# Score and activation matmuls as chained 64-row halves, banks by name, score copies on ScalarE

## The chip, the cores and the metric

The kernel runs on one core of one Trainium2 chip. The metric is the device time of one execution in microseconds, the median of three runs. The profiled execution is a run of its own. It has a span, from the first to the last instruction, and its own time, which takes in what lies around the span.

## The reference, cut to what matters

Two branches over the same input x (2048 tokens, 576 features) are mixed by a gate. Branch a is a long convolution with a kernel K that is generated from complex parameters (576 channels, 128 states). Branch b is a product-key expert layer: scores of 32 heads against 2 x 64 keys, the two best of each, a softmax over the two best pairs, and for the chosen experts a GELU of x·u, which weighs rows of v.

```python
g = sigmoid((x * gate_w).sum(-1, keepdims=True))
# a: K[d, l] = Re sum_n C dt B exp(l dt A);  y = irfft(rfft(u) * rfft(K))[:L] + u * Dskip
# b: 4096 experts = 64 x 64
s1 = einsum("nhd,ed->nhe", q1, k1); s2 = einsum("nhd,ed->nhe", q2, k2)
i1, i2 = two best of s1, two best of s2
top_s, top_e = two best of the four sums t1 + t2
act = gelu(einsum("nd,nhkd->nhk", x, u[top_e]))
b = einsum("nhk,nhk,nhkd->nd", softmax(top_s), act, v[top_e])
out = g * a + (1 - g) * b
```

## The kernel before

The program is written out by a planner: a model clock advances with each matmul that `mm` (L214) records, generators for every side task lie on a heap and are run by `pump` when their time has come, and `ready` and `need` make them wait for a modelled result or a free buffer. The order in which instructions are recorded is the order of each engine's queue. ScalarE and VectorE calls go through `Engine.call` (L134), so almost every row names one of those two lines.

**Score groups** (`s`, 128 of them). The key matrices are folded into the query weights, which gives 4096 score columns. A group is one of 8 column blocks of 512 by one of 16 tiles of 128 tokens. Both operands are split into a high and a low fp16 part (three products: high-high, high-low, low-high). `triple` records four contraction steps of 128 rows with three products each, and two matmuls for the last 64 features, whose high and low parts are stacked in one 128-row operand; half of the second one's rows are zero. That is 14 matmuls of 512 columns in one accumulation bank. `scores_top` then runs 8 MAX8 and 8 FIND_INDEX8 on VectorE, straight from the bank.

**Activation groups** (`a`, 128 of them) are the same for x·u: 8 blocks of 512 experts, 4 token blocks, 4 parts. `act_post` scales the bank into `go` and stores it.

The main loop takes a score group when VectorE's modelled lag is small enough and a bank is free, otherwise an activation group. It holds the last 26 activation groups back while score groups remain.

**The second path** runs beside it. `k_params`, `k_factors` (wbp), `k_front` (kP, phases), `k_gen` (kb) and `k_store` make the convolution kernel, 16 channels at a time. `u_stage1` makes the first stage of the input's transform, `k_stage1` (k) that of the kernel, `products` (pr, pi, pv) multiplies in the frequency domain. Then `gating` and `v_work` (vhl, the split expert table) finish what the output stage needs.

**The output stage.** For each token tile `prep` builds one-hot matrices on VectorE, PE places the gates (S), and 192 matmuls of 288 columns (o) sum over the experts; `y_part` adds the convolution.

**Banks.** There are eight accumulation banks. `bank` takes a place from a quota (sc for groups, kb and wb for the second path) and a tile from one ring of eight:

```python
def bank(tag, name):
    take(tag, name)
    t = ps.tile([128, 512], F32, tag="ps", name=name, bufs=8)
```

At the start the quotas are sc=4, kb=4; after the kernel generation sc=4, wb=4; during the products sc=3, wb=5. All DMAs are issued by SyncE in recorded order.

Of the kernel before, what the change touches and what calls it, by code (L numbers as in the profile page):

```python
# [18 lines left out]
OP = mybir.AluOpType  # L19
# [19 lines left out]
KB = 4  # L39
RA = 2 * CH * R1  # L40
# [98 lines left out]
def body(ctx: ExitStack, tc: tile.TileContext, xT, au, par, logdt, dskip, gatew, wq, kT, uT, vv,  # L139
# [67 lines left out]
    def mm(o, l, r, start, stop, cost=None):  # L207
        m = l.shape[0] > 64, 128 if size(l) > 64 else size(l)
        if m != tiling[0]:
            tiling[0] = m  # L210
            clock[0] += 0.13 if m == (True, 128) else 0.1
        clock[0] += (size(r) * (4 if r.dtype == F32 else 1) / 2400 + 0.003) if cost is None else cost
        rdy[key(o)] = clock[0] + 0.4
        T.matmul(o, l, r, start=start, stop=stop)  # L214
# [26 lines left out]

    def wait(gen):
        for t in gen:
            idle(t)

    slots, caps, owed = {}, {}, {}

    def quota(**kw):
        for tag, n in kw.items():
            lst = slots.setdefault(tag, [])  # L250
# [10 lines left out]
    def need(tag, n=1):  # L261
        while True:
# [10 lines left out]
    def free(tag, *outs):  # L273
# [14 lines left out]
    quota(sc=4, wb=0, kb=4, hw=1, slot=9, go=3, m8=2, raw=1, ko=1)  # L288
# [153 lines left out]
    def squares(a, r, sq, dst):  # L442
# [8 lines left out]
        mm(p[:, 0:2], onesb, short(acc[0].start, 2), True, True, 0.05)  # L451
        yield from ready(p)
        V.tensor_reduce(out=dst, in_=p[:, 0:2], axis=AX, op=OP.add)
        free(tag, dst)
# [5 lines left out]
    def x_norm(tb, sq):  # L460
# [15 lines left out]
        free("kb", nx)  # L476
# [23 lines left out]
    def scale_first(a, r, sq, keep=None):  # L500
# [16 lines left out]
        free("kb", out[0])  # L517
        return out

    def x_build(tb):  # L520
# [32 lines left out]
        V.scalar_tensor_tensor(b[64:128, 8], r[64:128], s[64:128], b[64:128, 8], op0=OP.mult, op1=OP.subtract)  # L553
        free("slot", b)
        xb.append(b)
        if tb == 3:
            V.tensor_reduce(out=nx2, in_=nx, axis=AX, op=OP.max)
            yield from ready(nx2)
            open_u()
# [38 lines left out]
    def w_half(c, h, w):  # L598
# [17 lines left out]
        for n in range(2):  # L616
            mm(p[:, 0:1], onesb, short(acc[n].start, 1), n == 0, n == 1, 0.03)
# [3 lines left out]
        free(tag, s)  # L621
# [19 lines left out]
    def w_tail(c, k, pb, hl, rem, o, count, s, tag):  # L641
        yield from ready(pb, s)
        if k < 4:
            yield from split(hl[:, 0, k:k + 2, o], hl[:, 1, k:k + 2, o], pb.rearrange("p (k n) -> p k n", k=2), s)
            free(tag, hl)
        else:
# [5 lines left out]
            for ps_, co in halves2:  # L652
                V.scalar_tensor_tensor(rem[0:64, 1, co], pb[ps_, 0:128], s[ps_], rem[ps_, 0, co],
                                       op0=OP.mult, op1=OP.subtract)
            free(tag, rem)
# [29 lines left out]
    def k_params():  # L685
# [7 lines left out]
        Zp = kg.tile([128, NCK, 6, CH], BF16, name="Zp")  # L693
# [74 lines left out]
        for h in range(2):  # L768
# [5 lines left out]
            free("kb", sc[:, b[h]])  # L774
# [5 lines left out]
        par_t.update(g=gN, a=aN, rt=rt[:, 0:RA // 2].bitcast(BF16), l2=rt[:, RA // 2:RA // 2 + R2], l1=rt[:, RA // 2 + R2:], Z=Zp)  # L780
# [4 lines left out]
    def k_factors(g):  # L785
# [3 lines left out]
        for k in range(KB):  # L789
            mm(p[:6 * CH, NS * k:NS * k + NS], par_t["Z"][:, KB * g + k], identb, True, True)  # L790
        yield from ready(p)
        t = kg.tile([6 * CH, KB, NS], BF16, tag="wb", name=f"wb{g}", bufs=2)
        copy(t.rearrange("p k n -> p (k n)"), p[:6 * CH])
        free("kb", t)
# [6 lines left out]
    def k_front(c):  # L801
# [18 lines left out]
        def reduce(z, p):  # L820
# [9 lines left out]
            free("kb", CS)  # L830
            left[0] -= 1

        for z in range(2):
# [4 lines left out]
            mm(p, wb_[:, c % KB, :], rt[0:6 * CH, 512 * z:512 * z + 512], True, True)  # L838
            spawn(reduce(z, p))
# [18 lines left out]
        for CS, e, ex in both:  # L858
            S.activation(e, e, AF.Exp)
            S.activation(ex, ex, AF.Exp)  # L860
        for d, (CS, e, ex) in enumerate(both, c - 1):
            v = CS.rearrange("p c s l -> p s c l")
            S.activation(v[:, 0:2], v[:, 0:2], AF.Sin, scale=-TWO_PI, bias=halfpi)
            S.activation(v[:, 2:4], v[:, 2:4], AF.Sin, scale=-TWO_PI)
# [48 lines left out]
    def k_store(c, kb):  # L913
# [9 lines left out]
        free("kb", ko)  # L923
# [4 lines left out]
        if kstored[0] == NCK:  # L928
# [3 lines left out]
            quota(sc=4, wb=4, kb=0, raw=2)  # L932
# [16 lines left out]

    tops = {}  # L950

    def scores_top(c, t, pb):
        yield from ready(pb)
        q = t % 4
        if q == 0:
            yield from need("m8")
            take("m8", "m8")
            tops[c, t // 4] = (xp.tile([128, 4, 8, 8], F32, tag="m8", name=f"m8_{c}_{t}", bufs=2),
                               xp.tile([128, 4, 8, 8], U32, tag="i8", name=f"i8_{c}_{t}", bufs=2))
        while (c, t // 4) not in tops:  # L960
            yield 0.3
        m8, i8 = tops[c, t // 4]
# [4 lines left out]
        free("sc", i8)  # L967
        seen[0] += 1
        if q == 3:
            yield from ready(i8)  # L970
            S.activation(vals[:, t - 3:t + 1, 8 * c:8 * c + 8, :], m8[:, :, :, 0:2], AF.Copy)
            S.activation(idx[:, t - 3:t + 1, 8 * c:8 * c + 8, :], i8[:, :, :, 0:2], AF.Copy)
# [71 lines left out]
    def turned(t, p):  # L1044
# [3 lines left out]
        free("wb", idxT)  # L1048
# [14 lines left out]
    def u_stage1():  # L1063
# [18 lines left out]
        def tail(p, tag, pbs):  # L1082
            for g in range(2):
                o = us[:, 2 + g, :]
                for hh in range(2):
                    pb = pbs[hh][g]
                    yield from ready(pb)
                    ov = o[:, 288 * hh:288 * hh + 288]
                    S.activation(ov, pb[:, :288], AF.Copy)
                    free(tag, ov)  # L1090
                yield from ready(ov)
                dma(pair_rows(su_d, 2 * p + g), o)
            ended[0] += 1

        load(0)
        for p in range(NT):
# [4 lines left out]
            h = uf.tile([128, 2, D], F16, tag="uh", name=f"uh{p}", bufs=2)  # L1101
# [10 lines left out]
            yield from need(tag, 4)  # L1112
            hungry[0] = False
            pbs = [[bank(tag, f"u1_{p}_{g}_{hh}") for g in range(2)] for hh in range(2)]
            for hh in range(2):
                cs = slice(288 * hh, 288 * hh + 288)
                for n, (z, w) in enumerate(((0, 0), (0, 1), (1, 0))):
                    for g in range(2):
                        r = slice(64 * g, 64 * g + 64)
                        mm(pbs[hh][g][:, :288], tu[r, z], h[r, w, cs], n == 0, n == 2, 0.063)  # L1120
            spawn(tail(p, tag, pbs))
            del pbs
# [11 lines left out]
    def k_stage1(ksb, fk, tabs):  # L1134
        enter, leave, count = ring(3)

        def tail(w, o, pbs):
# [702 lines left out]
```

## Time and profile before

| | |
|---|---|
| median of three runs | 1455.22 us (1452.94 to 1456.87) |
| profiled execution, own time | 1458.63 us |
| its span | 1456.8 us, 36814 instructions |
| PE busy | 1430.8 us (98%) |
| DVE busy | 1221.0 us (84%) |
| ACT busy | 776.0 us (53%) |
| POOL busy | 521.4 us (36%) |
| mean granted TensorE clock | 0.998 of 2.4 GHz |

An engine's busy time is the union of its instructions' records. A matmul's record is longer than its share of the engine, because matmuls are pipelined; the pitch from one start to the next tells what it costs. "A x12" in a timeline is a run of twelve records, its second number the time from the first start to the last end.

### The profile page before, as it was taken

The numbers are of one execution on the slowest core, as the hardware profiler recorded it, in microseconds if no ns is written. First come the engines' busy times: TensorE is split into PE (matmuls) and PEld (weight loads), VectorE is DVE, ScalarE is ACT, GpSimd is POOL, SyncE is SP. The second block draws the span as 40 slices with busy tenths as digits, with TensorE's granted clock in tenths as the row PEclk, the third lists the DMA queues.
The fourth block names the chain that finished last, engine by engine and source line by source line (L and its number), as shares of the span: only waits on it lengthen the run. The fifth ranks groups of instructions, "written<-read, shape, count | busy, mean of one in ns | idle before, by whom it ended". The sixth has DMA issues, their size and how long they took to land.

```text
span 1456.8 us, 36814 instructions
## 1 busy us (share of the span) xinstructions
PE 1430.8 (98%) x14103; PEld 853.9 (59%) x14105; DVE 1221.0 (84%) x4569; ACT 776.0 (53%) x1304; POOL 521.4 (36%) x510
## 2 busy tenths in 40 slices
PE   7999999999999999999999999999899999999998
PEld 3445445555454445455555444447687887888787
DVE  6898889889877996885989898689998988998860
ACT  6346776796685776834556564576333224323310
POOL 0335357536446446210237999623000100110100
PEclk9999999999999999999999999999999999999999
DMA  8235223442434432269486776787343432342400
GB/s 306 77 112 172 88 80 109 126 138 72 129 106 124 116 104 92 62 211 292 157 304 216 266 250 214 255 265 228 130 122 110 140 120 98 125 148 67 157 9 17
DMA packets 134352, 215.44 MB, mean 148 GB/s; under 512 B 10912, under 2 KB 79904, under 8 KB 127776
## 3 DMA queue, kind: packets, MB, share of 16 engines
q1 hardware_dynamic: 134080, 213.01, 45.3%
q8 instruction: 111, 1.82, 0.5%
q14 instruction: 65, 0.53, 0.1%
q10 hardware_dynamic: 96, 0.07, 0.0%
HBM read 141.74 MB, written 71.30 MB: 146 GB/s over the span
## 4 chain that ended last, share of the span: by engine, by line
PE 85%; DVE 5%; DMA 2%; ACT 1%; issue 0%; POOL 0%; SPq 0%; DVEq 0%; POOLq 0%
PE o L214 25%; PE s L214 22%; PE a L214 22%; PE S L214 4%; PE kb L214 2%; PE wb L214 2%; PE pr L214 2%; DMA vn<-in_au_dram 1%; PE y L214 1%; PE kP L214 1%; PE k L214 1%; DVE i L134 1%; PE pv L214 1%; PE u L214 1%; DVE vhl L134 1%; DVE m L134 1%
## 5 line engine op out<-in xcount | busy, mean ns | idle before, releaser
L214 PE MATMUL o<-vhl,wh 128*128 128x288 f16 x3072 | 389.2, 287 | 0.0
L214 PE MATMUL s<-whl,xb 128*128 128x512 f16 x1536 | 365.0, 379 | 0.0
L214 PE MATMUL a<-xb,uhl 128*128 128x512 f16 x1536 | 359.5, 379 | 0.2 <-DVE go L134 0.2
L214 PEld LDWEIGHTS <-wh 128*128 128x128 f16 x3072 | 296.8, 98 | 77.5 <-issue 3.7
L214 PEld LDWEIGHTS <-xb 128*128 128x128 f16 x1792 | 170.6, 98 | 208.5 <-issue 14.3
L214 PEld LDWEIGHTS <-uhl 128*128 128x128 f16 x1536 | 147.1, 98 | 176.3 <-issue 3.2
L134 DVE FIND_INDEX8 i<-m,s 128x8 uint32<-128x64 f32 x1024 | 206.9, 226 | 0.0
L134 ACT ACTIVATE wh<-gl,s_wg 128x1024 f16<-128x1024 f32 x64 | 69.0, 1137 | 203.6 <-DVE gl L134 203.6
L134 DVE MAX8 m<-s 128x8 f32<-128x64 f32 x1024 | 146.4, 217 | 27.1 <-PE s L214 26.6
L134 POOL TENSOR_TENSOR CS<-CS,ex 128x512 f32<-128x512 f32 x72 | 97.9, 1389 | 147.6 <-DVE ex L134 146.2
L134 POOL TENSOR_TENSOR ya<-ya,db 128x576 f32<-128x576 f32 x16 | 31.8, 1995 | 320.3 <-DVE Bg L134 159.2
L134 ACT ACTIVATE go<-a,i_a 128x512 f32<-128x512 f32 x92 | 61.5, 682 | 89.1 <-PE a L214 63.9
L134 DVE TENSOR_TENSOR gl<-S,gl 128x256 f32<-128x256 f32 x256 | 90.3, 416 | 13.5 <-PE S L214 10.1
L134 POOL TENSOR_TENSOR e<-aN,rt 128x512 f32<-128x512 f32 x72 | 83.1, 1174 | 49.9 <-PE kb L214 43.8
L134 DVE SCALAR_TENSOR_TENSOR wh<-gl,s_wg,wh 128x1024 f16<-128x1024 f32 x64 | 91.1, 1455 | 11.3 <-ACT wh L134 11.3
L134 DVE TENSOR_TENSOR Bg<-Be,vals 128x1024 f16<-128x1024 f16 x128 | 91.7, 758 | 2.2
L134 ACT ACTIVATE gl<-gl 128x1024 f32<-128x1024 f32 x64 | 63.4, 1044 | 34.1 <-DMA gl<-g_d 34.1
L214 PE MATMUL S<-Bg,A 128*128 128x64 f16 x2048 | 73.6, 194 | 6.4 <-DVE Bg L134 6.4
L214 PEld LDWEIGHTS <-A 128*128 128x128 f16 x2048 | 71.4, 98 | 11.4 <-DVE Bg L134 4.9
L134 DVE TENSOR_TENSOR A<-iota_a,vals 128x2048 f16<-128x2048 f16 x64 | 77.9, 1218 | 0.0
L134 DVE MATCH_VALUE_LOAD i<-m,s 128x8 f32 x1024 | 76.3, 75 | 0.1
L214 PE MATMUL s<-wrem,xb 128*128 128x512 f16 x256 | 76.2, 379 | 0.0
(206 smaller groups left out, 2156.6 us busy)
## 6 DMA issues: line engine op xcount, KB each, us to landing
g_d<-go SPq DMA_DIRECT2D x128, 256.0 KB, 2.4
gl<-g_d SPq DMA_DIRECT2D x32, 1024.0 KB, 5.5
wq<-in_wq_dram SPq DMA_DIRECT2D x16, 1152.0 KB, 5.6
su_d<-us SPq DMA_DIRECT2D x32, 288.0 KB, 2.6
sk_d<-k1o SPq DMA_DIRECT2D x32, 288.0 KB, 3.7
vn<-in_vv_dram SPq DMA_DIRECT2D x32, 288.0 KB, 4.1
ui<-su_d SPq DMA_DIRECT2D x16, 576.0 KB, 4.0
ki<-sk_d SPq DMA_DIRECT2D x16, 576.0 KB, 5.5
```

The source lines that it names most:

```text
L134: return f(*a, **k)
L214: T.matmul(o, l, r, start=start, stop=stop)
```

## The change

Score and activation groups are recorded as two lists of 64-row matmuls: the upper 64 partitions and the lower 64 (27 together). A queue `upper` and a list `lower` are served in ticks by `row_slot`: one matmul of an upper half, then one of a lower half of an earlier group. Both halves of a group add into the same bank. The lower half may start once more than LAG = 3 ticks have gone by since its upper half's last matmul, and an explicit wait for that matmul stands ahead of it. Consecutive groups alternate between even and odd token blocks, whose remainder part lies in opposite halves (14 + 13 and 13 + 14).

```diff
+    def row_slot():
+        tick[0] += 1
+        cost = 0.0
+        if upper:
+            g = upper[0]
+            o, l, r, start, stop = g["up"].popleft()
+            cost = size(r) / 2400 + 0.003
+            g["last"] = mm(o, l, r, start, stop, cost)
+            if not g["up"]:
+                upper.popleft()
+                g["end"] = tick[0]
+                lower.insert(sum(x["short"] for x in lower) if g["short"] else len(lower), g)
+        now = [g for g in lower if tick[0] - g["end"] > LAG or not upper]
+        if now:
+            g = now[0]
+            o, l, r, start, stop = g["low"].popleft()
+            if g["last"] is not None:
+                tc.add_manual_dep(T.nop().ins, g["last"].ins.name, ...)
+                g["last"] = None
+            mm(o, l, r, start, stop, max(0.0, size(r) / 2400 + 0.003 - cost))
...
+    def halved(pb, hl, rem, x, tb, tok, cols, x_first):
+        parts = []
+        for z in range(2):
+            h = slice(64 * z, 64 * z + 64)
+            lst = []
+            for k in range(4):
+                for xk, w in ((k, 0), (k, 1), (4 + k, 0)) if x_first else ((k, 0), (4 + k, 0), (k, 1)):
+                    lst.append((x[h, xk, tok], hl[h, w, k, cols]))
+            for n in range(1 + (z == tb % 2)):
+                lst.append((x[h, 8, tok], rem[h, n, cols]))
```

The remainder's low part is now written to all 128 partitions, so `w_tail` does four subtractions of 64x128 where it did two, and `u_build` one over 128 partitions.

Other matmuls go through the same queue as short groups ahead of the others (`first=True`): the norm sums (`total`: sq, wn), the factor transposes (wbp), the phases kP (96 rows before, 128 rows now, half each) and the stage k. They are done when their lower half is.

```diff
-                for n in range(2):
-                    mm(pb[:, :288], tkt[:, w % 16, n], ksb[:, 2 * hh:2 * hh + 2, :, w, :]..., n == 0, n == 1)
+                gs.append(rows(*([(pb[:, :288], tkt[h:h + 64, w % 16, n],
+                                   ksb[h:h + 64, 2 * hh:2 * hh + 2, :, w, :]...,
+                                   h == 0 and n == 0, h == 64 and n == 1) for n in range(2)] for h in (0, 64)), first=True))
```

Banks have names: each of the eight is a tile of its own, and `bank` takes the one that the planner expects to be free first, whatever set it was used by. The quotas become counts: sc=5, kb=3 once x is built; sc=5, wb=4 after the kernel generation; sc=4, wb=5 during the products. `u_stage1` takes two banks at a time where it took four.

```diff
-        take(tag, name)
-        t = ps.tile([128, 512], F32, tag="ps", name=name, bufs=8)
+        held[tag] += 1
+        b = min(vacant)
+        vacant.remove(b)
+        t = ps.tile([128, 512], F32, tag=f"ps{b[1]}", name=name, bufs=1)
```

When VectorE is late, ScalarE copies a score bank into one of now four `go` buffers, and VectorE searches the copy:

```diff
+        if V.free > clock[0] + 1.5 and S.free < V.free and sum(x <= clock[0] for x in slots["go"]) >= 2:
+            take("go", "sx")
+            x = actp.tile([128, 4, 128], F32, tag="go", name=f"sx{c}_{t}", bufs=4).rearrange("p t n -> p (t n)")
+            S.activation(x, pb, AF.Copy)
+            free("sc", x, of=pb0)
```

In `k_front` the exponentials and sines wait until ScalarE's modelled queue is at most 0.7 us long (`turn`), in place of being recorded all at once.

The main loop serves the upper queue first. When it is empty, it looks for a next group among the first eight of each list, one of the other parity if there is one; when no group can start, it serves the lower list alone:

```diff
+        if upper:
+            row_slot()
+            continue
...
+        if lower:
+            row_slot()
+            continue
         idle(0.3)
```

The order of the groups changes accordingly (two token blocks in turn), and the results of eight token tiles are gathered in other sets of four. The four first activation groups and the output stage are recorded as before.

## Rows read from the trace of the kernel before

**Rows 1.** Stages: length, busy time and count of PE, PEld, DVE, ACT, POOL, clock, DMA.
```profile
100.00:640.00 540.00, 536.94 (x5270) 267.71 (x5269) 467.94 (x2033) 381.21 (x568) 272.76 (x222) 1.00 0.36 109
...
750.00:900.00 150.00, 148.06 (x1451) 72.44 (x1449) 136.50 (x862) 83.13 (x232) 126.54 (x149) 1.00 0.69 238
...
1050.00:1456.80 406.80, 402.71 (x4595) 325.80 (x4591) 320.36 (x514) 111.46 (x112) 23.85 (x12) 1.00 0.32 101
```

**Rows 2.** PE's groups by shape: count, busy us, mean ns of one record, idle before.
```profile
L214 PE MATMUL s<-whl,xb 128*128 128x512 f16 x1536 | 365.0, 379 | 0.0
...
L214 PE MATMUL s<-wrem,xb 128*128 128x512 f16 x256 | 76.2, 379 | 0.0
...
L214 PE MATMUL wbp<-identb,Zp 128*96 128x128 bf16 x36 | 3.6, 221 | 0.0
L214 PE MATMUL wn<-sc,onesb 128*128 128x1 bf16 x32 | 3.1, 165 | 0.0
```

**Rows 3.** Timeline of PE around a burst of u: start, length, run.
```profile
353.33 2.11 PE L214 MATMUL s<-whl,xb 128*128 128x512 f16 x9
355.37 0.91 PE L214 MATMUL u<-uh,tu 64*128 64x288 f16 x12
356.21 0.82 PE L214 MATMUL s<-whl,xb 128*128 128x512 f16 x3
```

**Rows 4.** Tiles kb, k, pv, vhl, u: count, shortest, median and longest ns, first and last start.
```profile
L214 PE MATMUL kb<-Y,CS x1152: 219/219/244, 164.4 to 636.9; 128*32 128x64 f32 x192
...
L214 PE MATMUL k<-ksb,tk x128: 282/286/286, 678.7 to 744.2; 128*128 128x288 f16 x128
...
L214 PE MATMUL pv<-vf,cst x288: 376/376/427, 771.3 to 930.5; 64*64 64x256 f32 x144
...
L134 DVE SCALAR_TENSOR_TENSOR vhl<-vs,sci,vhl x3: 807/1952/1973, 1016.6 to 1021.3; 128x576 f16<-128x576 f32 x3
...
L214 PE MATMUL u<-uh,tu x192: 279/283/294, 96.6 to 633.6; 64*128 64x288 f16 x192
```

**Rows 5.** Waits: who waited for whom, us in total, times, longest.
```profile
POOL CS L134 <- DVE ex L134: 146.2, 17, 15.2
```

**Rows 6.** Timeline of PE at the start of the output stage.
```profile
993.94 0.59 PE L214 MATMUL a<-xb,wrem 128*128 128x512 f16 x2
...
995.34 2.37 PE L214 MATMUL o<-vhl,wh 128*128 128x288 f16 x18
...
1019.53 3.84 PE L214 MATMUL o<-vhl,wh 128*128 128x288 f16 x30
1027.94 0.23 PE L214 MATMUL S<-Bg,A 128*128 128x64 f16 x1 [4.57 <-DVE Bg L134]
```

**Rows 7.** Timeline of PE around wbp, wn and k.
```profile
130.45 0.39 PE L214 MATMUL wbp<-identb,Zp 128*96 128x128 bf16 x4
130.67 0.59 PE L214 MATMUL a<-xb,wrem 128*128 128x512 f16 x2
...
300.97 0.19 PE L214 MATMUL wn<-sc,onesb 128*128 128x1 bf16 x2
301.03 0.81 PE L214 MATMUL a<-xb,uhl 128*128 128x512 f16 x3
...
680.81 0.65 PE L214 MATMUL k<-ksb,tk 128*128 128x288 f16 x4
681.30 0.81 PE L214 MATMUL s<-whl,xb 128*128 128x512 f16 x3
```

**Rows 8.** Groups of DVE and of ACT by line.
```profile
L134 DVE SCALAR_TENSOR_TENSOR wrem<-wb,sci,wrem 64x128 f16<-64x128 f32 x32 | 11.1, 347 | 4.0 <-ACT wrem L134 3.8
...
L134 ACT ACTIVATE go<-a,i_a 128x512 f32<-128x512 f32 x92 | 61.5, 682 | 89.1 <-PE a L214 63.9 <-issue 22.4 <-DMA g_d<-go 2.3
```

**Rows 9.** Timeline of all engines at the end of an activation group.
```profile
301.67 0.59 PE L214 MATMUL a<-xb,wrem 128*128 128x512 f16 x2
...
302.30 0.75 DVE L134 TENSOR_SCALAR go<-a,i_a 128x512 f32<-128x512 f32 x1 [0.22 <-PE a L214]
```

More of the change, by code (lines that the diff above doesn't have):

```diff
@@ L2 @@
 import math
+from collections import deque
 from contextlib import ExitStack
@@ L39 @@
 KB = 4
+LAG = 3
 RA = 2 * CH * R1
@@ L213, in mm, with rows, total @@
         rdy[key(o)] = clock[0] + 0.4
-        T.matmul(o, l, r, start=start, stop=stop)
+        return T.matmul(o, l, r, start=start, stop=stop)
+    upper, lower = deque(), []
+    tick = [0]
+    def rows(up, low, then=None, first=False):
+        g = {"up": deque(up), "low": deque(low), "then": then, "done": False, "end": None, "short": first}
+        (upper.appendleft if first else upper.append)(g)
+        return g
+    def row_slot():
[15 more added lines that the diff above has]
+            if g["last"] is not None:
+                tc.add_manual_dep(T.nop().ins, g["last"].ins.name,
+                                  mybir.DependencyInfo(mybir.DependencyClass.Sync, mybir.DependencyReason.DATA),
+                                  reason="the lower half of the rows follows the upper half in a bank")
+                g["last"] = None
+            mm(o, l, r, start, stop, max(0.0, size(r) / 2400 + 0.003 - cost))
+            if not g["low"]:
+                lower.remove(g)
+                g["done"] = True
+                if g["then"]:
+                    g["then"]()
+    chained = [False]
+    def total(p, cols):
+        n = len(cols)
+        if not chained[0]:
+            for k, x in enumerate(cols):
+                mm(p, onesb, x, k == 0, k == n - 1, 0.03)
+            return
+        hs = slice(0, 64), slice(64, 128)
+        g = rows(*([(p, onesb[h], x[h], z == 0 and k == 0, z == 1 and k == n - 1) for k, x in enumerate(cols)]
+                   for z, h in enumerate(hs)), first=True)
+        while not g["done"]:
+            yield 0.2
     def spawn(gen, after=0.0):
@@ L240, in ready, with turn @@
             yield t
+    def turn(e, late):
+        while e.free > clock[0] + late:
+            yield e.free - clock[0] - late
     def wait(gen):
@@ L246, in body @@
     slots, caps, owed = {}, {}, {}
+    banksets = "sc", "kb", "wb"
+    held = dict.fromkeys(banksets, 0)
+    vacant = [(0.0, n) for n in range(8)]
+    number = {}
     def quota(**kw):
         for tag, n in kw.items():
+            if tag in banksets:
+                caps[tag] = n
+                continue
             lst = slots.setdefault(tag, [])
@@ L261, in need @@
     def need(tag, n=1):
+        while tag in banksets:
+            lst = sorted(vacant)
+            if held[tag] + n <= caps[tag] and len(lst) >= n and lst[n - 1][0] <= clock[0]:
+                return
+            yield max(0.2, min(0.3, lst[n - 1][0] - clock[0])) if len(lst) >= n else 0.3
         while True:
@@ L271, in take, with free @@
         lst.remove(min(lst))
-    def free(tag, *outs):
+    def free(tag, *outs, of=None):
+        if of is not None:
+            held[tag] -= 1
+            vacant.append((max([clock[0]] + [rdy.get(key(x), 0.0) for x in outs]), number[of.tensor.name]))
+            return
         if owed[tag]:
@@ L615, in w_half @@
         p = bank(tag, f"wn{c}_{h}")
-        for n in range(2):
-            mm(p[:, 0:1], onesb, short(acc[n].start, 1), n == 0, n == 1, 0.03)
+        yield from total(p[:, 0:1], [short(a.start, 1) for a in acc])
         yield from ready(p)
@@ L788, in k_factors @@
         p = bank("kb", f"wbp{g}")
[L789 to L790 removed]
+        Z = par_t["Z"]
+        parts = []
+        for h in range(2):
+            hs = slice(64 * h, 64 * h + 64)
+            parts.append([])
+            for k in range(KB):
+                o = 6 * CH * (KB * g + k)
+                parts[-1].append((p[:, NS * k + 64 * h:NS * k + 64 * h + 64], Z[hs, o:o + 128],
+                                  identb[hs, 64 * h:64 * h + 64], True, True))
+        w = rows(*parts, first=True)
+        while not w["done"]:
+            yield 0.2
         yield from ready(p)
[L792 to L794 removed]
+        t = kg.tile([128, KB, NS], BF16, tag="wb", name=f"wb{g}", bufs=2)
+        copy(t.rearrange("p k n -> p (k n)"), p)
+        free("kb", t, of=p)
         par_t[g] = t
@@ L1080, in load, with tail @@
             ld[p] = a, tu
-        def tail(p, tag, pbs):
+        def tail(p, hh, tag, pbs):
             for g in range(2):
                 o = us[:, 2 + g, :]
[L1085 to L1093, printed above, removed]
+                pb = pbs[g]
+                yield from ready(pb)
+                ov = o[:, 288 * hh:288 * hh + 288]
+                S.activation(ov, pb[:, :288], AF.Copy)
+                free(tag, ov, of=pb)
+                if hh:
+                    yield from ready(ov)
+                    dma(pair_rows(su_d, 2 * p + g), o)
+            ended[0] += hh
         load(0)
@@ L1135, in k_stage1, with tail @@
         enter, leave, count = ring(3)
-        def tail(w, o, pbs):
+        def tail(w, o, pbs, gs):
+            while not all(g["done"] for g in gs):
+                yield 0.2
             yield from ready(*pbs)
@@ L1713, in body @@
             pump()
-    del acts[0:4]
+    for j in range(4):
+        acts.remove((0, 0, j))
+        used(("u", 0), ("x", 0))
     if 0 in i_u:
@@ L1757, in body @@
+            if g:
+                groups.remove(g)
+                start_group(g)
+                continue
+        if a_ok and bank_free():
+            acts.remove(a)
+            start_group(a)
+            continue
+        if lower:
+            row_slot()
+            continue
         idle(0.3)
+    while upper or lower:
+        row_slot()
+        pump()
+    chained[0] = False
     until(lambda: min(stored) == 32 and shut)
```

251 lines of the change are left out of this document (154 added, 97 removed).

## The prediction

> **What bounds the kernel now.** The stage table comes first [rows 1]. The 64-row change lives in the stretch up to 1000 us, where the score and activation groups run. TensorE is busy 536.94 of 540 us from 100 to 640 us, 148.06 of 150 from 750 to 900, at full granted clock. From 1050 us on it is busy 402.71 of 406.8, with work that the change leaves alone. So instructions on PE set the time, and a PE instruction fewer is worth its pitch as long as nothing else becomes late. The second view is PE's groups by shape [rows 2]: 14 matmuls of 512 columns in each score group (12 x 128 + 2 x 128 = 1536 + 256 records), and the activation groups are built alike. The third is the order of time [rows 3]: nine such matmuls take 2.11 us, the last record 0.379, so the pitch is (2.11 - 0.38) / 8 = 0.216 us, one column a cycle. There is no slack inside a group.
>
> Other engines are close behind. DVE is busy 467.94 of 540 us (87%) and 136.50 of 150 (91%), POOL 126.54 of 150 between 750 and 900 [rows 1]. The last view is a second path beside PE. The convolution kernel's matmuls (kb) run from 164 to 637 us, the next stage 679 to 744, the products end at 930, and the last piece of the expert table is scaled at 1021 to 1023 [rows 4]. POOL waited 146.2 us in 17 waits on DVE in that path [rows 5], not on PE. At the joint the two meet: PE finishes its activation groups at 994.5, starts the output stage at once, and at 1023.4 stands for 4.57 us on DVE [rows 6]. So the second path has no more than about 5 us to give.
>
> **The change part by part.**
>
> *The chain.* A contraction of 3 x 576 = 1728 rows is 13.5 array heights; before it takes 14. As 27 half-height matmuls, upper and lower half side by side, it takes 13.5 ticks if the halves really overlap. The trace has that form: the 64-row matmuls of u, two halves in two banks. Twelve take 0.91 us, the last record 0.283 [rows 3], so six pairs go at (0.91 - 0.28) / 5 = 0.125 us a pair, and 288 columns are 0.120 us at a column a cycle. Two halves cost what one full matmul costs, weight loads included. 256 groups less the first 4, which stay as they are: 252 x 0.5 x 0.216 = **-27.2 us**.
>
> *Mode changes.* Entering u, the score matmuls should hand over at 353.33 + 9 x 0.216 = 355.27 and u starts at 355.37; leaving, 355.37 + 6 x 0.125 = 356.12 against 356.21 [rows 3]. That is 0.2 us a burst, and beside a chain of the same row halves it goes: 192 / 12 = 16 bursts [rows 4] x 0.2 = **-3.2 us**. Bursts of 32 and 64 columns still change the mode as before: 0.
>
> *Short groups in the chain.* Norm sums (wn), the factor transposes (wbp) and the stage k are now halves too and sit beside 512-column partners. Before, a pair of wn cost 300.97 to 301.03 = 0.06 us, four wbp 0.22, four k 0.49 [rows 7]. No row shows a short half beside a long one. From above, each takes a whole tick: for the four k, 8 ticks of which half the array does useful work, 8 x 0.216 x 0.5 = 0.86, +0.37 x 32 (128 / 4 [rows 4]) = 11.9; for wn (32 / 2 [rows 2]) 0.43 - 0.06 = 0.37 x 14 (of 16, two come before the chain) = 5.2; for wbp 0.86 - 0.22 = 0.64 x 9 (36 / 4 [rows 2]) = 5.8; together +22.9. From below, shorts meet shorts, as in u: 0. I take **+14**, a little above the middle, because k comes in dense runs that can meet one another, wn and wbp do not. The Trainium skill (TensorE: Matmul & The Clock Gate, section Part 3: Packing small matmuls) says that matmuls start and end in program order even on different row halves. By that no short one slips past its long partner and the term is +22.9; the trace's pairs, equal in length, agree but cannot show it.
>
> *Filling and draining.* When no group can start, one half runs alone and each such tick loses 0.108 us. A full stop loses 17 ticks at each side (13 or 14 plus the lag), 34 x 0.108 = 3.7 us. Before, PE stood idle only 3.1 us from 100 to 640 and 1.9 from 750 to 900 [rows 1]. A bank is now held by PE for 14 + 4 + 13 = 31 ticks, 6.7 us, against 3.0; five banks of 2.9 us a group leave 14.5 - 6.7 = 7.8 us for the reader, where four left 12.1 - 3.0 = 9.1. The ScalarE copy (about 0.68 us, as the go row [rows 8]) gives a bank back when DVE is late, so I take one stop, **+4**. Bounds: 0, and a tenth of the 3402 ticks alone, +37.
>
> *The wait between the halves.* One wait a group stands in PE's order, everything behind it waits too. It comes four ticks, 0.86 us, after the start of the matmul that it waits for. The last activation matmul's record ends at 302.26 and DVE starts on it at 302.30 [rows 9], 0.42 us after that matmul's start (302.26 - 0.38). So it is open when PE gets there: 0. If PE cannot prepare weights past it, one hidden load per group shows, estimated at no more than the 0.1 us of a mode change: 252 x 0.1 = +25 is the other end.
>
> *Beside PE.* 32 more remainder subtractions at 0.347 us [rows 8] are +11 us on DVE, which has 72 us idle between 100 and 640 [rows 1]; copies of at most 128 groups x 0.68 = 87 us on ACT, idle 159 us there. Hidden; without that cover the 11 us would show. Whether MAX8 is quicker or slower from the copy no row shows; as PE is the bound I take 0. SP's queue gets no more DMAs. The banks by name remove waits on a ring, but PE shows no such wait: 0.
>
> *Sum.* -27.2 - 3.2 + 14 + 4 = -12.4 us on PE. At the joint the second path can give about 5 us without moving itself. Its own start is paced by the loop that issues the groups, and groups that take less PE let it come round sooner, but not fully; I give up 2.4 us there: **-10**. The profiled execution took 1458.6 us (span 1456.8), 3.4 above the median of 1455.2; it becomes 1448.6, and the median 1445.
>
> **Rivals.**
> 1. *All of it.* Shorts fall beside shorts and the second path follows: -27.2 - 3.2 + 4 = -26, 1429. For it: u's perfect pairs. Against: 87 to 91% DVE.
> 2. *Whole ticks.* The short groups at their upper end: -12.4 + 8.9 = -3.5, 1452. For it: PE issues in order, and the planner in the diff charges a tick at the longer half. This is the time by the rule of the Trainium skill cited above; no run yet shows an unequal pair.
> 3. *The second path holds.* It stays where it is: products bound by POOL (84% busy), the last vhl at 1023, then the wait at 1023.4 [rows 1, 4, 6]. Only the 4.57 us can be won: 1451 to 1455, say 1453. Against it: before, its first part waits in DVE's queue, which the groups fill.
> 4. *Slower: the convolution kernel starves.* Its banks go from 4 to 3, and a kP result now needs an upper tick, four of lag and a lower tick, some 5 ticks or 1.1 us more. The path has 18 bursts of kb (1152 / 64) from 164 to 637 [rows 4]. At 1.1 us for each that isn't hidden by running ahead: 18 x 1.1 = 20 us, less the 5 to spare at the joint, +15: 1470. It decides from 0.3 us a burst. For it: DVE and POOL are already waited for there [rows 5]. Against: the front part of each burst runs some blocks of channels ahead. Halves running alone for 8% of the ticks would end at a similar time.
>
> That the halves don't overlap at all (27 x 0.216 a group) is excluded by u.
>
> **How the numbers follow.** Forecast 0.38, rival 1 0.17, rival 2 0.10, rival 3 0.11, rival 4 0.24. A difference under 0.3% (4.4 us) cannot be told from none. Faster: 0.33 of the forecast, all of rival 1, 0.03 each of 2 and 3: 0.56. Within: 0.05 + 0.06 + 0.07 + 0.01 = 0.19. Slower: 0.25, nearly all rival 4. The forecast's own range is 1437 to 1451; to leave out only two in ten it must reach rival 1 and most of rival 4: 1427 to 1469.
>
> **What would show it.** Right: 27 half records a group in place of 14, pairs 0.216 us apart; u without the 0.1 us at each side; the output stage starting 8 to 14 us earlier. Short groups: gaps beside wn and k of one tick or none. Rival 3: an activation group that ends early, then PE idle before the first output matmul. Rival 4: the last kb later than 637. Wrong altogether: long stretches with one half alone, or a gap at each wait.

## The result and the profile after

The changed kernel takes 1463.36 us (median of six runs, 1462.18 to 1464.81) where the kernel before took 1456.6 beside it: ratio 1.0048, 95% interval 1.0033 to 1.0063. It is slower by half a per cent; forecast were 10 us less. The profiled execution has a span of 1462.0 us and 44130 instructions; the mean granted clock of TensorE is 0.991.

The stages of the changed kernel, with the columns of [rows 1]: PE is as full as before, ScalarE has taken on 50 us in the first stretch, and the stretch from 1050 us to the end is 5.2 us longer.

```profile
100.00:640.00 540.00, 535.60 (x7402) 308.27 (x7400) 461.27 (x2184) 430.95 (x689) 263.87 (x217) 1.00 0.35 108
750.00:900.00 150.00, 148.19 (x1886) 71.36 (x1880) 139.71 (x792) 99.54 (x277) 135.58 (x159) 1.00 0.75 259
1050.00:1462.00 412.00, 408.36 (x4673) 330.71 (x4670) 326.56 (x524) 116.71 (x118) 24.47 (x12) 1.00 0.31 101
```

PE's groups by shape, as [rows 2]: 3072 + 384 score records are 27 half matmuls for each of 128 groups. The norm sums and the factor transposes are halves too, 60 and 72 records.

```profile
L216 PE MATMUL s<-whl,xb 64*128 64x512 f16 x3072 | 466.0, 377 | 0.1
L216 PE MATMUL s<-wrem,xb 64*128 64x512 f16 x384 | 123.1, 376 | 0.0
L216 PE MATMUL wn<-sc,onesb 64*128 64x1 bf16 x60 | 6.3, 163 | 0.1
L216 PE MATMUL wbp<-identb,Zp 64*128 64x64 bf16 x72 | 5.7, 190 | 0.0
```

The timeline of PE round a burst of u, as [rows 3]. The 0.1 us at each side of u is gone, and something else is to be seen. Three u start at 302.15, then (0.40 - 0.28 = 0.12 later) 302.27, and at 302.39, 0.12 us apart: 288 columns on one half of the rows. After them that half runs a-matmuls from 302.51. Only then, at 302.57, the other half starts its three u. The program writes the six in turn, one for each half. So the halves slip past one another by some matmuls.

```profile
302.15 0.40 PE L216 MATMUL u<-uh,tu 64*128 64x288 f16 x2
302.36 0.38 PE L216 MATMUL a<-xb,uhl 64*128 64x512 f16 x1
302.39 0.28 PE L216 MATMUL u<-uh,tu 64*128 64x288 f16 x1
302.51 0.38 PE L216 MATMUL a<-xb,uhl 64*128 64x512 f16 x1
302.57 0.40 PE L216 MATMUL u<-uh,tu 64*128 64x288 f16 x2
302.73 0.38 PE L216 MATMUL a<-xb,uhl 64*128 64x512 f16 x1
302.82 0.28 PE L216 MATMUL u<-uh,tu 64*128 64x288 f16 x1
```

PE in stage k, as [rows 7]. Halves of k (288 columns) start 0.10 to 0.12 us apart beside score halves that keep their 0.21 (686.51, 686.72, 686.94):

```profile
686.51 0.38 PE L216 MATMUL s<-whl,xb 64*128 64x512 f16 x1
686.61 0.28 PE L216 MATMUL k<-ksb,tk 64*128 64x288 f16 x1
686.72 0.38 PE L216 MATMUL s<-whl,xb 64*128 64x512 f16 x1
686.73 0.40 PE L216 MATMUL k<-ksb,tk 64*128 64x288 f16 x2
686.94 0.38 PE L216 MATMUL s<-whl,xb 64*128 64x512 f16 x1
```

The end of an activation group, as [rows 9]: the last half's record ends at 305.41 and DVE starts 0.04 us later, as before.

```profile
305.03 0.38 PE L216 MATMUL a<-xb,wrem 64*128 64x512 f16 x1
...
305.45 0.75 DVE L136 TENSOR_SCALAR go<-a,i_a 128x512 f32<-128x512 f32 x1 [1.17 <-PE a L216]
```

The tiles of the second path, as [rows 4]. kb starts 16 us later and ends 14 later, k and the products (pv) end 16 us earlier, the last piece of the expert table 9 us later. u is done 150 us sooner.

```profile
L216 PE MATMUL kb<-Y,CS x1152: 219/219/243, 180.3 to 650.6; 128*32 128x64 f32 x192
L216 PE MATMUL k<-ksb,tk x256: 279/282/293, 684.5 to 728.6; 64*128 64x288 f16 x128
L216 PE MATMUL pv<-vf,cst x288: 376/376/427, 759.3 to 914.4; 64*64 64x256 f32 x144
L136 DVE SCALAR_TENSOR_TENSOR vhl<-vs,sci,vhl x3: 801/804/1958, 1024.4 to 1030.2; 128x576 f16<-128x576 f32 x3
L216 PE MATMUL u<-uh,tu x192: 279/283/293, 91.8 to 482.1; 64*128 64x288 f16 x192
```

Who waited for whom: us, times, longest. The first line answers to [rows 5]. The others are PE's; the wait on issue, those of k and the one of tr are longer than any of their kind before.

```profile
POOL CS L136 <- DVE ex L136: 167.6, 18, 29.2
...
PE S L216 <- DVE Bg L136: 7.9, 6, 3.1
PE kb L216 <- issue: 3.3, 1, 3.3
PE k L216 <- ACT k1o L136: 2.4, 2, 2.2
PE k L216 <- DVE m L136: 1.9, 1, 1.9
PE tr L216 <- DVE vals L136: 1.2, 1, 1.2
```

The start of the output stage in PE's timeline, as [rows 6]. The first output matmul starts at 996.59, 1.25 us later than before, not 8 to 14 earlier. PE then stands for DVE for more than a microsecond at three places in place of one.

```profile
996.59 0.91 PE L216 MATMUL o<-vhl,wh 128*128 128x288 f16 x6
999.24 0.19 PE L216 MATMUL S<-Bg,A 128*128 128x64 f16 x1 [1.75 <-DVE Bg L136]
...
1030.34 1.39 PE L216 MATMUL o<-vhl,wh 128*128 128x288 f16 x10 [1.22 <-DVE vhl L136]
1034.86 0.23 PE L216 MATMUL S<-Bg,A 128*128 128x64 f16 x1 [3.14 <-DVE Bg L136]
```

Two stretches of the changed kernel in which the granted clock is half (seventh column, 1.2 of 2.4 GHz). Each begins at the end of a wait of PE or within 2 us behind it, 3.29 us on issue and 1.23 on vals. Three more, 955 to 959, 1000 to 1003 and 1034 to 1041, begin in the same way at waits on Bg (1.82, 1.75 and 3.14 us). Before, only 1027.6 to 1034.5 was slow while PE worked, at the end of the 4.57 us of [rows 6].

```profile
597.00:600.50 3.50, 3.19 (x16) 1.18 (x17) 1.15 (x2) 2.75 (x3) 2.73 (x3) 0.51 0.19 70
921.00:928.00 7.00, 7.00 (x74) 3.85 (x76) 2.88 (x11) 5.60 (x17) 0.75 (x1) 0.52 1.01 362
```

DVE's and ScalarE's groups, as [rows 8]: the remainder subtractions doubled at the same 347 ns, and MAX8 from a ScalarE copy (sx) takes 81.4 / 592 = 0.138 us of DVE against 61.7 / 432 = 0.143 from the bank. 74 of 128 score groups were copied, 597 ns each.

```profile
L136 DVE MAX8 m<-sx 128x8 f32<-128x64 f32 x592 | 81.4, 207 | 6.2 <-ACT sx L136 5.9
L136 ACT ACTIVATE sx<-s 128x512 f32<-128x512 f32 x74 | 44.2, 597 | 29.1 <-PE s L216 28.1 <-issue 1.1
L136 DVE MAX8 m<-s 128x8 f32<-128x64 f32 x432 | 61.7, 214 | 24.2 <-PE s L216 20.0 <-PE u L216 3.5 <-PE k L216 0.5
L136 DVE SCALAR_TENSOR_TENSOR wrem<-wb,sci,wrem 64x128 f16<-64x128 f32 x64 | 22.2, 347 | 1.2 <-ACT wrem L136 0.3
```

### The profile page after: what moved, and what is told of

Its sections match the earlier page's. It is cut to its first block, busy times and chain, and to the rows that moved or that the text cites. A ratio compares the mean times of both kernels' runs of the same rounds, so it can differ in the third digit from the quotient of the medians.

```text
span 1462.0 us, 44130 instructions
## 1 busy us (share of the span) xinstructions
PE 1426.9 (98%) x17654; PEld 901.9 (62%) x17654; DVE 1199.1 (82%) x4559; ACT 848.8 (58%) x1477; POOL 527.5 (36%) x515
## 5 line engine op out<-in xcount | busy, mean ns | idle before, releaser
L216 PE MATMUL s<-whl,xb 64*128 64x512 f16 x3072 | 466.0, 377 | 0.1
L216 PE MATMUL a<-xb,uhl 64*128 64x512 f16 (+1 forms) x3024 | 458.0, 378 | 0.7 <-ACT uhl L136 0.3
L216 PEld LDWEIGHTS <-xb 64*128 64x128 f16 x3456 | 222.1, 94 | 167.5 <-issue 14.8
L216 PEld LDWEIGHTS <-uhl 64*128 64x128 f16 (+1 forms) x3024 | 196.4, 94 | 167.0 <-issue 8.9
L216 PE MATMUL s<-wrem,xb 64*128 64x512 f16 x384 | 123.1, 376 | 0.0
L216 PE MATMUL a<-xb,wrem 64*128 64x512 f16 (+1 forms) x380 | 120.7, 377 | 0.0
L136 DVE FIND_INDEX8 i<-m,sx 128x8 uint32<-128x64 f32 x592 | 116.5, 215 | 0.0
L136 DVE TENSOR_TENSOR gl<-S,gl 128x256 f32<-128x256 f32 x256 | 90.3, 414 | 16.4 <-PE S L216 10.0
L136 DVE SCALAR_TENSOR_TENSOR wh<-gl,s_wg,wh 128x1024 f16<-128x1024 f32 x64 | 89.6, 1428 | 14.2 <-ACT wh L136 14.1
L136 DVE FIND_INDEX8 i<-m,s 128x8 uint32<-128x64 f32 x432 | 87.0, 220 | 0.0
L136 DVE MAX8 m<-sx 128x8 f32<-128x64 f32 x592 | 81.4, 207 | 6.2 <-ACT sx L136 5.9
L136 DVE MAX8 m<-s 128x8 f32<-128x64 f32 x432 | 61.7, 214 | 24.2 <-PE s L216 20.0
```

Of the source, the lines that this page charges most:

```text
L136: return f(*a, **k)
L216: return T.matmul(o, l, r, start=start, stop=stop)
```

## The experiments

My theory after the result (A): the chain does shorten PE's work, and the rest of the change, or waits that it brings, eat it. Its rivals: the second path sets the end whatever PE does (B), or the chain itself costs more than it saves (C). All ratios are to the kernel before, run beside them, with 95% intervals. Where the text does not say that the order is kept, the planner writes the program anew: the order of all instructions shifts, and some copies and scalings can go to another engine, because the planner gives them to the one that it expects to be free. Such a difference is that of the part and of the new order together.

### Parts of the change taken out

**No chain**: in `start_group` the branch of full-height groups is always taken; wbp, kP and k are written as 128-row matmuls.

```diff
-        if caps["sc"] < 4:
+        if True:
```

> The changed kernel with the chain taken out: groups, factor transposes, kP and stage k are 128-row matmuls again; banks by name, score copies, ScalarE turns and the new order of groups stay. Theory A (the chain shortens PE's work by about 9 us before the output stage and the rest of the change costs the time): slower than the changed kernel, about 1472. Theory B (the second path through DVE, POOL and ScalarE sets when the output stage can run, whatever PE does): within 3 us of the changed kernel, 1460 to 1466, with the wait at the joint as long. Theory C (the chain itself costs more than it saves, by its lone ticks and edges): back at the kernel before, 1455 to 1458.

**No copies**, with the chain, and **neither**:

```diff
-        if V.free > clock[0] + 1.5 and S.free < V.free and sum(...) >= 2:
+        if False and sum(...) >= 2:
```

> The changed kernel with ScalarE's copies of score banks off; DVE reads every score from its bank. Theory A and C: the chain holds a bank for 31 ticks, so without copies PE waits for banks: slower than the changed kernel, 1466 to 1480. Theory B: the copies put 74 x 0.6 = 44 us of work on ScalarE beside the second path; without them the path is earlier at the joint: 1455 to 1460.

> Neither chain nor copies; of the change only banks by name, ScalarE turns, the new order of groups and the padded factors are left. If these small parts are neutral: 1453 to 1459 as before. If one of them moves the second path (theory B in its other form): 1460 or more, with kb starting near 180 us as in the changed kernel.

| | with copies | without |
|---|---|---|
| chain | 1.0048 (the change) | 1.0317 [1.0298, 1.0336] |
| no chain | 1.0083 [1.0065, 1.0101] | 1.0274 [1.0255, 1.0292] |

Without the copies the changed kernel is 39 us slower. With both out it is 40 us slower than before; kb then starts at 193 us. With the chain it is 5 us faster where the copies are in and 6 slower where they are out. So what is left (banks by name, the new order of groups, the turns of ScalarE, three banks in place of four for the convolution kernel), as the planner then writes it, is by far not neutral. That fits A best, but the run without copies says that no part has a worth by itself, and how much of the 39 us is the copies' and how much the new order's was not tested.

**Four banks for the convolution kernel again**, and **the old order of groups**:

```diff
-            quota(sc=5, kb=3)
...
-            quota(sc=5, wb=4, kb=0, raw=2)
+            quota(sc=4, wb=4, kb=0, raw=2)
```

> The changed kernel with the bank counts of before: four banks for the convolution kernel and four for the groups, chain and copies kept. If the convolution kernel starves on three banks (rival 4): kb starts near 164 us in place of 180, 1445 to 1455. If the fifth bank is what the chain lives on: longer PE idle times, 1470 to 1490. If neither: 1460 to 1467.

```diff
-    groups = [(c, 8 * p + 4 * z + k) for c in range(8) for p in range(2) for k in range(4) for z in range(2)]
+    groups = [(c, t) for c in range(8) for t in range(NT)]
...
-        near = [g for g in lst[:8] if ok(g)]
+        near = [g for g in lst[:1] if ok(g)]
```

> The changed kernel with the groups in the order of before (one token block after the other, so that neighbours in the chain have the longer half on the same side). The chain then loses a tick at each joint of two groups: PE up to 252 x 0.1 = 25 us more, but gating of a head needs its token blocks in the old order. If the new order is what moved the second path: kb, k or the products 10 us earlier or more and 1450 to 1458. If not: 1466 to 1485.

1.0105 [1.0083, 1.0127] and 1.0218 [1.0195, 1.0241]. With four banks kb ends where it did before, yet the output stage starts at 1017.3:

```profile
L216 PE MATMUL kb<-e,CS x1152: 219/219/243, 176.8 to 636.4; 128*32 128x64 f32 x192
...
L216 PE MATMUL o<-vhl,wh x3072: 283/286/297, 1017.3 to 1467.5; 128*128 128x288 f16 x192
```

The run takes the bank from the groups, which had five, so it does not price the starving by itself. More is said against my rival 4 by the changed kernel's own trace: its sign is there (the last kb 14 us later), but k and the products end 16 us earlier than before, so the late kb did not reach the joint. With the old order of groups the changed kernel is 25 us slower.

**The copies alone, added to the kernel before** (four buffers, `scores_top` as in the change):

> The kernel before with the score copies by ScalarE alone (four buffers for them, one u buffer less), no chain, old banks, old order. The theory that the output stage waits for a second path in which DVE's queue is the scarce thing: score banks come free sooner, 1440 to 1452. The theory that the copies only repair what the bank rules of the change break: 1454 to 1462.

1.0088 [1.0067, 1.0108]. The part without which the changed kernel is 39 us slower makes the kernel before slower too. Neither of the expected answers fits. The next runs ask what a new order does by itself.

### The order by itself

**The kernel before with another price in its planner.** `mm` adds 0.12 and 0.09 in place of 0.13 and 0.1 us to the clock by which the program is written. The work and the matmuls are the same. Their order changes, and some forty copies and scalings change their engine: DVE is busy 1230.6 us where it was 1221.0.

```diff
-            clock[0] += 0.13 if m == (True, 128) else 0.1
+            clock[0] += 0.12 if m == (True, 128) else 0.09
```

> The kernel before, same work and same instructions; only the price that the planner sets for a change of matmul shape is 0.12 and 0.09 in place of 0.13 and 0.10 us, so the written order of the instructions shifts. If the time follows the amount of work: 1453 to 1460, as before. If it follows how the order happens to fall at the joint: another time by 10 us or more, in either direction.

1.0255 [1.0232, 1.0277], 37 us with no change of the work to be done. The 9.6 us more on DVE are a part of what the new order brings, and were not tested apart. The products end 29 us later, and at the joint PE has run out of groups and stands 10.36 us for DVE:

```profile
L214 PE MATMUL pv<-vf,cst x288: 376/376/427, 799.3 to 959.9; 64*64 64x256 f32 x144
...
1017.42 0.24 PE L214 MATMUL S<-Bg,A 128*128 128x64 f16 x1 [10.36 <-DVE Bg L134]
```

**The kernel before with 13 matmuls a group**, once with the order that the planner then writes, once with every other engine's order kept. This is the edit of the second, in which the 14th is priced, but not issued:

```diff
-            mm(pb, l, r, False, n == 1)
+            mm(pb, l, r, False, True, emit=n == 0)
```

> The kernel before with the 14th matmul of each score and activation group left out (the low half of the remainder is not added): 252 x 0.216 = 54 us less work on PE and no other change. If PE's work reaches the end: 1400 to 1410. Theory B: the second path holds the output stage and PE waits at the joint: 1440 to 1452, which bounds what any saving of the chain's 27 us could bring.

> The kernel before with every other engine's instructions in exactly its order, and the 14th matmul of each group not issued: 54 us less PE work (the low half of the remainder is left out). Where the same cut with a new order gave 1472. If PE's work reaches the end as long as the order stands: 1400 to 1415. If the second path holds the output stage in any order: 1446 to 1453.

With 54 us less on PE the first is slower, 1.0098 [1.0077, 1.0118]; the second is 35 us faster, 0.9757 [0.9736, 0.9777]. The same work, 50 us apart (DVE is busy 1236.0 us in the first and 1219.8 in the second, for the reason given above). The stretch from 900 to 1000 us, first with the new order, then with the old one: in the new one PE idles 26 of 100 us, at a lower clock, waiting for DVE.

```profile
900.00:1000.00 100.00, 73.92 (x820) 40.39 (x812) 78.53 (x161) 59.73 (x121) 53.44 (x55) 0.84 0.83 276
```

```profile
900.00:1000.00 100.00, 93.30 (x928) 58.11 (x926) 89.83 (x140) 66.71 (x105) 29.80 (x20) 0.98 0.82 261
```

After the first of the two I believed theory B. The second takes it back: where the order stands, most of what PE saves comes through. Half as much less, and as much more, in the same order:

> The kernel before in its own order with the 14th matmul left out in every second group: 27 us less PE work, what a perfect chain would have saved. With 54 us less, 35 came through. If savings come through in proportion (0.65): 1440. If the first microseconds come through whole and the second path takes the later ones: 1430 to 1434. If the joint takes the first ones: 1446 to 1452.

> The kernel before in its own order with the 14th matmul of each group issued twice: 54 us more work on PE (it adds the low half of the remainder twice). If PE alone set the time: 1510. If the second path held by itself: well under that, 1480 to 1500.

0.9853 [0.9831, 0.9874] for 27 us less, and 1.0302 [1.0285, 1.0320] for 54 us more. In us of the kernel before (ratio times 1458): -21 of 27, -35 of 54, +44 of 54.

### The chain by itself, with the order kept

Every entry of the chain is priced and placed as in the changed kernel; what TensorE is given is a 128-row matmul where the upper half stood, and nothing where the lower half stood. DVE, ScalarE, GpSimd and the queues have the changed kernel's order to the last instruction.

```diff
-            g["last"] = mm(o, l, r, start, stop, cost)
+            mm(o, l, r, start, stop, cost, False)
+            for _ in range(1 if g["up"] else len(g["full"])):
+                if g["full"]:
+                    fo, fl, fr = g["full"].popleft()
+                    T.matmul(fo, fl, fr, ...)
```

> The changed kernel with every instruction of DVE, ScalarE, GpSimd and the queues in exactly the changed kernel's order, but TensorE issues 128-row matmuls in place of each chain pair (14 a group, and whole short groups) where the upper halves stood. Theory A (the chain saves about 10 us on PE and PE's work reaches the end): 1471 to 1480, 10 us or more above the changed kernel's 1463. Theory B (the written order of the second path sets the end): 1460 to 1467. If the chain itself loses time: under 1460.

> As the run with the changed kernel's order and 128-row matmuls, but 13 a group: 54 us less PE work than with 14 and 27 less than a perfect chain (the low half of the remainder is left out). If a better chain could have paid in this order: 1430 to 1440. If the second path holds: 1452 to 1462.

Full height 1.0052 [1.0032, 1.0071], with 13 matmuls 0.9838 [0.9816, 0.9860]. So the chain is worth nothing that can be told here (1.0048 against 1.0052), while 54 us less brought 31 in the same order.

The same pair in another order, the one of the 0.12 price:

> The changed kernel with the planner's price for a change of matmul shape at 0.12 and 0.09 us, as was done to the kernel before (there +37 us): same work, another written order. If the changed kernel's 1463 is one draw among orders that differ by tens of us: another time by 10 us or more, in either direction. If the chain makes the order robust: 1460 to 1467.

> The changed kernel in the order that the other planner price gave (1471.7 with the chain), with 128-row matmuls in place of the pairs. If the chain's worth is about 2 us in any order: 1471 to 1476. If it depends on the order: outside, 1460 to 1470 or 1477 to 1490.

1.0086 [1.0067, 1.0106] with the chain, 1.0131 [1.0116, 1.0147] without: there it is worth 0.45%, 6.6 us (the two profiled executions, 1472.25 and 1474.05 us, are 1.8 apart). So the chain gives 0 to 7 us by the order, and the changed kernel's order was the better one of two.

**Only the groups as pairs**, the short ones full height in their upper place:

```diff
-            g["last"] = mm(o, l, r, start, stop, cost)
+            g["last"] = mm(o, l, r, start, stop, cost, not g["short"])
```

> The changed kernel in its own order, with the score and activation groups as chain pairs but the short groups (factor transposes, kP, norm sums, stage k) as 128-row matmuls where their upper halves stood. They took 6.5 us more as halves than whole (k 5.7 of it). If they are what spoils the chain: 1455 to 1458. If the long groups' chain loses what it gains at its many interruptions: 1461 to 1465, as the changed kernel.

1.0486 [1.0469, 1.0503], by the ratios 64 us slower than the changed kernel, and a miss of both theories. The timeline shows why: each short matmul now leaves a long half alone in its own tick and in the one of its lower half.

```profile
302.09 0.23 PE L241 MATMUL wbp<-identb,Zp 128*128 128x128 bf16 x1
302.25 0.39 PE L218 MATMUL a<-xb,uhl 64*128 64x512 f16 x1
302.57 0.23 PE L241 MATMUL wbp<-identb,Zp 128*128 128x128 bf16 x1
302.73 0.39 PE L218 MATMUL a<-xb,uhl 64*128 64x512 f16 x1
303.05 0.23 PE L241 MATMUL wbp<-identb,Zp 128*128 128x128 bf16 x1
```

One wbp and one lone half take 302.57 - 302.09 = 0.48 us. 72 kP, 128 k, 36 wbp and 30 wn are 266; two lone halves for each are 266 x 2 x 0.108 = 57 us, the size of what the long groups lose (next section's sum: 766.0 to 823.7; the changes of shape are in it). The short halves inside the chain were the right choice.

**Another order for each kernel**, chosen for an early end on the planner's own clock:

```diff
-        ... 2.0 if not turn_s else 5.0 ...   # kernel before
+        ... 3.0 if not turn_s else 5.0 ...   # and yield 14, v_norm at 20
-        turn_s = ... < 8 + 1.25 * ...        # changed kernel
+        turn_s = ... < 10 + 1.25 * ...       # and 5.0 for 6.0, 0.12 for 0.13
```

> The kernel before, same work, with three of its rules of order changed: a score group may start with DVE 3 us behind in place of 2, the u bursts stand 14 us apart in place of 12, and the gate's norm starts 20 us earlier. If the order of before was one of the best of its kind: 1458 to 1480. If it was not: 1445 to 1454.

> The changed kernel, same work, with three rules of order changed: price of a shape change 0.12 in place of 0.13 us, a score group may start with DVE 5 us behind in place of 6, and scores take their turn two groups earlier against activations. If the chain needs only another order to pay: 1445 to 1456. If its missing microseconds are its own: 1459 to 1475.

1.0051 [1.0037, 1.0065] and 1.0043 [1.0029, 1.0056]. No version that computes all of it has beaten the kernel before. The five other orders that the planner wrote for full-height matmuls and all of the work (no chain, neither, copies alone, other price, this one) lie 0.5 to 2.7% above it.

## Why the prediction was wrong

The total of the PE sum was near, its terms were not. For each PE record before the first output matmul I take the time from its start to the next one's start, less what lies beyond its end, and add it up by tile. Full height and chain in the same order:

| us | full height | chain | difference | predicted |
|---|---|---|---|---|
| score and activation groups | 785.4 | 766.0 | -19.4 | -27.2 + 4 |
| u | 15.4 | 14.1 | -1.3 | -3.2 |
| k, kP, wn, wbp | 34.6 | 42.4 | +7.7 | +14 |
| sum | 835.5 | 822.5 | -13.0 | -12.4 |
| idle behind a record | 12.5 | 19.3 | +6.8 | 0 |
| all others and the start | | | +4.1 | 0 |
| start of the output stage | 998.7 | 996.6 | -2.1 | |

That -13.0 stands beside -12.4 is in part luck: the long groups and u together bring 5.7 us less than forecast, and the short groups cost 6.3 less. The forecast was also for another start, the kernel before. There the same three rows come to 831.8 us, so the change takes 9.3 off. Most of the difference to 13.0 the change had first added itself: `u_stage1` with two banks makes 32 bursts of six u where before had 16 of twelve, and at full height the changes of shape at their sides cost 3.0 us more.

*The chain, filling and draining.* 3.0 of the 19.4 us are the steps into u, which this count puts down to the record ahead of u. So the chain itself brought 16.4 of 27.2 us, and 10.8 are lost, not 4. The clock has a good part of it: 8.4 us of these groups' time lie in stretches at half clock (the full-height run has none before its output stage), which makes 4.2 us, an estimate. The other 6.6 are halves that run alone, where other shapes cut the chain into 88 stretches (counted in the trace), the edges of these stretches, and a few waits between the halves; they were not parted. The wait is free as forecast, and pairs start 0.216 us apart, save at some ten places where the upper queue was empty and the lower half comes right behind its upper one (`or not upper` in `row_slot`). There the next start is 0.42 to 0.47 us later, some 2.5 us lost in all:

```profile
300.36 0.38 PE L216 MATMUL kP<-rt,wb 64*128 64x512 bf16 x1
...
300.83 0.39 PE L216 MATMUL kP<-rt,wb 64*128 64x512 bf16 x1
```

*Short groups.* +7.7 in place of +14, of it k 5.6 and wn 1.1; kP, which I had left out, 0.9; wbp nothing. By the Trainium skill's rule that matmuls start in program order (TensorE: Matmul & The Clock Gate, Part 3: Packing small matmuls) the estimate was 22.9. The trace does not agree: the u at 302.15 to 302.82 start out of program order between the halves, and halves of k start 0.12 us apart beside score halves at 0.21. So a short half need not wait for a long partner.

*The step that failed* is the last one, "I give up 2.4 us there: **-10**", together with "*Beside PE.*" and its "PE shows no such wait: 0". It gave up 2.4 of 12.4 us between PE and the output stage, and put the rest of the change at nothing. Two things stand in its place.

First, the other parts of the change are not free. With 128-row matmuls as before they cost 0.52%, 7.6 us. About 3 of it are, by the count above, the shorter bursts of u. The load of the engines does not explain the rest: ScalarE is busy 842.4 us of 1463 in place of 776.0, DVE 1201.1 in place of 1221.0. The parts change the order in which everything is written, and a new order, with the copies that it moves between engines, was worth 37 us with no work changed, and 50 with 54 us of work removed. That the order is the rest of the 7.6 us is argued from these sizes; no run has the parts in the order of before. I had priced instructions and held their order fixed; the forecast is the answer to another question. For that question it was a fair one: 27 us less PE work, in before's order, brought 21.

Second, of the 13 us only 2.1 reach the output stage: 10.9 are given up, not 2.4. 6.8 become idle time: 3.29 on issue in a kb burst that has no such wait at full height, and longer waits at k, tr and Bg. Most of the other 4.1 lies in the products, transposes and S (pr +1.7, tr +0.9, S +0.8). The clock is at half for some 13.6 us before the output stage, and at full height in every stretch up to 1000 us it was granted as 1.00; half of 13.6, an estimate of some 7 us, is lost by that, 4.2 of it in s and a, 1.6 in tr. That the waits cause the falls fits every fall, but was not tested alone: a wait of 2.2 us at 720.7 brought none.

Against the kernel before, the -9.3 us meet +7.3 of idle time and +3.2 in all other matmuls and the start, and the output stage begins 1.25 us later. It then takes 4.0 us more, though the change leaves its work alone: PE waits 1.5 us more in it, and the clock is at half for 10.2 us of it in place of 6.8.

*The rivals.* "All of it" failed on both counts. "Whole ticks" had too little slip. "The second path holds" is refuted as a law (54 us less brought 35 in the old order and 31 in the changed kernel's). "The convolution kernel starves" was the slower side, with the right sign at kb, but the path made the delay up before the joint: k and the products end 16 us earlier than before. What I lacked was a rival that says: a new order is likelier worse than that of the kernel before, as all were that the runs above tried with the full work.

What stays open: which steps of the order at the joint decide. The runs show where it ends (PE waiting for Bg and vhl; DVE is busy 97% from 1000 to 1050 us, but was 96% before), not which early choice puts DVE there.

## What to carry over

Where a planner writes the order, ask first how far the time moves when the work stays and the order is new; here that was more than any term of the sum. Then test the edit with the order kept, by pricing the old instruction and issuing the new one: that separates its own worth from the new order in two runs. In a chain of half-height matmuls count the ticks in which a half runs alone, at the price of a pair, and let no full-height matmul stand among them.

## What the runs showed of the hardware

The two row halves keep no common order: one was some two long matmuls ahead of the other at 302 us.

PE, ScalarE and DVE all stood at 594 to 597 us behind a burst of kb, with no releaser in the trace. Two views of the changed kernel, first the burst and the gap behind it, then the instruction queue from 590 to 600 us (packets, MB, share of 16 engines). The DMA engines are full in the burst (1.04), hardly anything computes but GpSimd in the gap, and the instruction queue moves two packets. That the engines waited for instructions behind that traffic is argued, not tested. The kernel before has one of 1.65 us at 455.9, also with the DMA engines full ahead of it.

```profile
590.00:593.80 3.80, 3.80 (x146) 2.54 (x143) 1.82 (x3) 2.00 (x2) 3.80 (x5) 1.00 1.04 310
593.80:597.30 3.50, 0.22 (x15) 0.06 (x4) 0.00 (x0) 0.00 (x0) 2.78 (x3) 0.96 0.45 151
```

```profile
q8 instruction: 2, 0.03, 1.2%
```
